# Writing out TensorE's and ScalarE's order in the weight fold of a recurrent-attention and mixture-of-experts kernel

## The chip, the core and the metric

The kernel runs on one core of a Trainium2 chip. The metric is the device time of one execution in microseconds (us), as the median of several runs.

## The reference

Three layers follow one another. The second has two matrices behind its product, and nothing between them, which is what the kernel's "fold" uses.

```python
# 1. recurrent attention, r,k,v,w: (4, 8, 768, 48), u: (8, 48)
for t in range(S):
    cur = einsum('bhd,bhe->bhde', u[None] * kt, vt)
    y[:, :, t] = einsum('bhd,bhde->bhe', rt, state + cur)
    state = wt[..., None] * state + einsum('bhd,bhe->bhde', kt, vt)
# 2. x: (3072, 384); w1, w2: (384, 1024); w3: (1024, 1024); w_out: (1024, 384)
x = (((x @ w1) * (x @ w2)) @ w3) @ w_out
# 3. eight experts, the best two of each token by noisy gate logits
logits = x @ w_gate + log1p(exp(x @ w_noise)) * noise
out[token] += weight[token, k] * (maximum(x @ e1[e], 0) @ e2[e])
```

## The kernel before, in words

**The fold.** w3 and w_out are multiplied with each other first: W = w3 @ [w_out | w_out @ (w_gate, w_noise)], 1024 rows of 400 columns. They arrive as 64-bit numbers. Every matrix is kept as a high and a low half, and a product takes three matmuls (`mm3`, lines 169 to 172: high x high at L170, high x low at L171, low x high at L172). W comes in two halves of four 128-row blocks; a half fills the PSUM banks PB[0] to PB[3] and is summed over eight blocks of w3, so there are sixteen blocks of w3, each with a set of twelve matmuls of 128x400 (`mm_w3`), and eight blocks of w_out.

**Conversion.** `cvt` (line 135) turns a loaded block into halves: ScalarE makes "top" (L145); a later `flush` (line 149) lets VectorE make the 32-bit number "z" (cvz, L154), ScalarE cast its high half "h" (L156), and the flush after that lets VectorE subtract to the low half "l" (L161). Each `cvt` calls `flush(1)` between its "top" and its entry into the queue; a flush first makes z and h of the block that waits and then l of the block before that.

**The gate exchange.** For each block of w_out TensorE transposes z (`wo_T`, L366), ScalarE copies the result out (woT, L368), TensorE multiplies it with the gate columns (`gate_cols`, L373), and ScalarE and VectorE split the 16 columns (`gate_split`, by `split`, L123 and L124). The set of block j needs both halves of these columns.

**Beside it.** A table `todo` holds steps by slot; pass u of the loop runs slot u - 24. In these slots lie the loads (`load_dt`, `load_na`, `load_w`, all issued by SP), the preparation of attention chunks 0 to 2 (`pre_steps`: pre_scan L193 on VectorE, pre_rec with Ln and Exp on ScalarE L202 and L203, further products on VectorE or POOL, pre_u on POOL L222 and L223, pre_c, and pre_d, eight ScalarE copies, L235), and chunks 0 and 1 themselves (`att_steps`: at_A L242 on TensorE, at_ov L247 on VectorE, at_T L252 with a ScalarE copy, at_kv L263 with sc and snew on VectorE L267 to L274 and the state's copies on ScalarE L278, at_y L302 with xh on ScalarE L308 and xl on VectorE L309). Slot -15 is that of chunk 0's pre_d and chunk 1's scan. Behind the loop the slots -5 to -1 follow, then the main loop over pairs of chunks, then the experts.

**What sets the order.** VectorE issues in the order in which the program is written, everywhere (line 78). The other engines' order is a planner's, made when the program is compiled: it takes the instructions by their place in the program and by when its model takes them to be ready, and so it may let a ready instruction pass one that waits. In the loop of lines 466 to 485 the set of block u - 3 is multiplied in pass u; the gate exchange of block u - 1 lies in pass u; W's first half is split in pass 10 at once, behind the eighth set.

Of the kernel before, what the change touches and what calls it, by code (L numbers as in the profile page):

```python
# [8 lines left out]
F32 = mybir.dt.float32  # L9
# [9 lines left out]
P = 128  # L19
B, H, S, D = 4, 8, 768, 48  # L20
DM, FF, E = 384, 1024, 8
# [8 lines left out]
XW = DM + 16  # L30
# [41 lines left out]
def tile_kernel(ctx: ExitStack, tc: tile.TileContext, dt, nat, w3t, wout, w1, w2, e1, e2, cf, ci, out):  # L72
    nc = tc.nc
    pe, act, dve, pool, sp = nc.tensor, nc.scalar, nc.vector, nc.gpsimd, nc.sync
# [6 lines left out]
    def f(ap):  # L81
        return ap.bitcast(F32)
# [17 lines left out]
    PB = [psum.tile([P, 512], F32, name=f"pb{i}") for i in range(8)]  # L100
# [9 lines left out]
    oneb = const.tile([P, P], BF16, name="oneb")  # L110
# [3 lines left out]
    att = attx.enter_context(tc.tile_pool(name="att", bufs=2))  # L114
# [4 lines left out]
    W0 = [wp.tile([P, 4, XW], F32R, name=x) for x in ("W0h", "W0l")]  # L119
    St = [att.tile([P, 4, 2 * D], F32, name=f"S{i}", bufs=1) for i in range(2)]  # L120

    def split(h, l, src, on=None):
        act.copy(out=h, in_=src)  # L123
        (on or dve).tensor_tensor(out=l, in0=src, in1=f(h), op=OP.subtract)  # L124
# [3 lines left out]
    def tops(n):  # L128

        pl, w, _ = CV  # L130
        TOP[:] = [pl.tile([P, w], I32, name=f"top{i}", bufs=1) for i in range(n)]
        for t in TOP:
            pool.memset(t, 0)
# [15 lines left out]
    def flush(n=2):  # L149
        for _ in range(n):  # L150
            low, LQ[:] = LQ[:], []
            while CQ:
                mid, t, z, h, l, post = CQ.pop()
                dve.scalar_tensor_tensor(z, mid, 13, t, op0=OP.logical_shift_right, op1=OP.bitwise_or)  # L154
                x = z.bitcast(F32)
                act.copy(out=h, in_=x)  # L156
                LQ.append((h, l, x))
                if post:
                    post(x)
            for h, l, x in low:  # L160
                dve.tensor_tensor(out=l, in0=x, in1=f(h), op=OP.subtract)  # L161

    def load64(rw, src):

        n = src.shape[-1]
        sp.dma_start(out=rw.bitcast(U16)[:, 1:4 * n + 1], in_=src.bitcast(U16))
        return rw[:, :2 * n + 2]

    def mm3(o, wh, wl, xh, xl, start, stop):
        pe.matmul(o, wh, xh, start=start, stop=False)  # L170
        pe.matmul(o, wh, xl, start=False, stop=False)  # L171
        pe.matmul(o, wl, xh, start=False, stop=stop)  # L172


    DT, NA, FG, RC, KT, RT, AM, KN, XH, XL, KS = ({} for _ in range(11))

    def load_dt(j):
        DT[j] = att.tile([P, NDT], F32, name="dtc")
        sp.dma_start(out=DT[j], in_=dt[j])
# [11 lines left out]
    def pre_scan(j):  # L191
        FG[j] = att.tile([P, 8 * (HC + 1)], F32, name="fg")
        dve.tensor_tensor_scan(out=FG[j], data0=DT[j][:, 8 * P:], data1=d1, initial=0.0,  # L193
                               op0=OP.mult, op1=OP.add)

    def pre_rec(j, step):

        fa = fgv(j)[:, :, 1:]
        if step == 0:
            RC[j] = att.tile([P, 8, HC], F32, name="rc", bufs=1)  # L200
            KT[j] = att.tile([P, 4, 2, HC], F32, name="kt")
            act.activation(out=RC[j], in_=fa, func=AF.Ln)  # L202
            act.activation(out=RC[j], in_=RC[j], func=AF.Exp, scale=-1.0)  # L203
        else:
            t = KT[j].rearrange("p a s i -> p (a s) i")
            off(j, 0).tensor_tensor(out=t, in0=fa, in1=RC[j], op=OP.mult)
            dve.scalar_tensor_tensor(RC[j], t, -2.0, RC[j], op0=OP.add, op1=OP.mult)

    def pre_k(j):
        k = DT[j][:, 4 * P:8 * P].rearrange("p (a s i) -> p a s i", s=2, i=HC)  # L210
        off(j, 1).tensor_tensor(out=KT[j][:, :, 0], in0=k[:, :, 0], in1=fgv(j)[:, 1::2, :HC], op=OP.mult)
        dve.scalar_tensor_tensor(KT[j][:, :, 1], k[:, :, 1], -1.0, RC[j][:, 0::2], op0=OP.mult, op1=OP.mult)

    def pre_r(j):
        RT[j] = att.tile([P, 4, 2, HC], F32, name="rt")
        r = DT[j][:, :4 * P].rearrange("p (a s i) -> p a s i", s=2, i=HC)
        dve.scalar_tensor_tensor(RT[j][:, :, 0], r[:, :, 0], -1.0, RC[j][:, 1::2], op0=OP.mult, op1=OP.mult)
        off(j, 2).tensor_tensor(out=RT[j][:, :, 1], in0=r[:, :, 1], in1=fgv(j)[:, 0::2, :HC], op=OP.mult)

    def pre_u(j):  # L220
        t = att.tile([P, DM], F32, name="rku", bufs=1)
        pool.tensor_tensor(out=t, in0=NA[j][:, :DM], in1=NA[j][:, DM:2 * DM], op=OP.mult)  # L222
        pool.tensor_tensor(out=t, in0=t, in1=c("u"), op=OP.mult)  # L223
        KS["u", j] = t

    def pre_c(j):
        t = KS["u", j]
        cc = att.tile([P, H], F32, name="cc")
        dve.tensor_reduce(out=cc, in_=t.rearrange("p (h d) -> p h d", h=H), axis=mybir.AxisListType.X, op=OP.add)
        KS["c", j] = cc  # L230

    def pre_d(j):
        AM[j] = att.tile([P, H, P], F32, name="am")
        for h in range(H):
            act.activation(out=AM[j][:, h], in_=ident, func=AF.Copy, scale=KS["c", j][:, h:h + 1])  # L235

    def at_A(j):
# [98 lines left out]
    def pre_steps(j):  # L336
        def p2():
            pre_k(j)
            pre_r(j)
            if j + 2 < NCH:  # L340
                load_dt(j + 2)

        return [lambda: pre_scan(j), lambda: pre_rec(j, 0), lambda: pre_rec(j, 1), p2, lambda: pre_u(j),
                lambda: pre_c(j), lambda: pre_d(j)]
# [4 lines left out]
    rawx, w3s, xo_, R1 = {}, {}, {}, {}  # L349
# [3 lines left out]
    def ld_raw(n=1):  # L353
        for _ in range(n):
            if order:
                k, u = order.pop(0)
                rawx[k, u] = load64(fold.tile([P, 1026], I32, name="rawf", bufs=7),
                                    wout[u] if k == "o" else w3t[u // 8, u % 8])

    def cv_wo(j):  # L360
        cvt(rawx["o", j], DM, woh[:, j, :DM], wol[:, j, :DM], post=lambda x: xo_.__setitem__(j, x))

    def wo_T(j):
        bank = PB[4 + j % 2]
        for kb in range(3):
            pe.transpose(bank[:, P * kb:P * kb + P], xo_[j][:, kb * P:kb * P + P], ident)  # L366
        xo_[j] = fold.tile([P, DM], F32, name="woT")
        act.copy(out=xo_[j], in_=bank[:, :DM])  # L368

    def gate_cols(j):  # L370
        g = bK[:, 256 + 32 * j:272 + 32 * j]
        for kb in range(3):
            pe.matmul(g, xo_[j][:, P * kb:P * kb + P], wgn[:, kb], start=kb == 0, stop=kb == 2)  # L373

    def gate_split(j):
        split(woh[:, j, DM:], wol[:, j, DM:], bK[:, 256 + 32 * j:272 + 32 * j])

    def cv_w3(u):
        w3s[u] = [fold.tile([P, 512], F32R, name=x, bufs=3) for x in ("w3h", "w3l")]
        cvt(rawx["3", u], 512, *w3s[u])  # L380

    def mm_w3(u):
        jb = u % 8
        for fb in range(4):
            s = slice(fb * P, fb * P + P)
            mm3(PB[fb][:, :XW], w3s[u][0][:, s], w3s[u][1][:, s], woh[:, jb, :], wol[:, jb, :], jb == 0, jb == 7)

    def load_w(m, fp):
        R1[m, fp] = load64(rawp.tile([P, 1538], I32, name="raw64"), (w1, w2)[m][fp])
# [19 lines left out]
    def at(slot, fn, *a):  # L409
        todo.setdefault(slot, []).append((fn, a))  # L410

    def run_todo(k):
        for fn, a in todo.pop(k, []):
            fn(*a)

    def start(j):
# [3 lines left out]
    PREL = {0: (-21, -20, -18, -17, -19, -16, -15), 1: (-15, -14, -13, -12, -14, -12, -11),  # L420
            2: (-10, -9, -4, -3, -6, -1, 0), 3: (1, 1, 4, 5, 3, 5, 6)}
# [16 lines left out]
            at(slot, cv_w, *k, i)  # L438
    for k, slot in WLD.items():
        at(slot, load_w, *k)  # L440
    for j in range(NCH):
        lo = ATT[j - 2][4] if 2 <= j < 6 else start(j - 2) + 4
        for i, fn in enumerate(pre_steps(j)):
            at(PREL[j][i] if j < 4 else max(lo, start(j) + PRE[i]), fn)
    for j in range(NCH):
        for i, fn in enumerate(att_steps(j)):
# [7 lines left out]
    ca = CF["u"][0]  # L454
    sp.dma_start(out=cft[:, :ca], in_=cf[:, :ca])
    ld_raw(6)
    tops(2)
    for t in St:
        pool.memset(t, 0.0)
# [1 line left out]
    pool.memset(d1.rearrange("p (a i) -> p a i", i=HC + 1)[:, :, :1], 1.0)  # L461
    pool.memset(zeros, 0.0)
    pool.memset(run, 0.0)
    pool.memset(oneb, 1.0)

    for u in range(19):
        if u < 8:
            cv_wo(u)
            ld_raw()
        if u < 16:  # L470
            cv_w3(u)
            ld_raw()
        elif u == 16:
            flush()
        if u > 2:
            mm_w3(u - 3)
        if 0 < u < 9:
            gate_cols(u - 1)
            gate_split(u - 1)
        if u < 8:  # L480
            wo_T(u)
        if u == 10:
            for fb in range(4):
                split(W0[0][:, fb], W0[1][:, fb], PB[fb][:, :XW])
        run_todo(u - 24)

    flush()
    foldx.close()
# [427 lines left out]
    if RMAX > 1:  # L916

        n = nc.values_load(rounds[0:1, E:E + 1], min_val=1, max_val=RMAX)  # L918
# [101 lines left out]
```

## Time and profile before

| | us |
|---|---|
| runs | 987.36, 987.98 (median), 988.5 |
| profiled execution, time | 987.58 |
| its span | 985.7 |
| TensorE busy (matmul) | 938.5 |
| VectorE busy | 444.7 |
| ScalarE busy | 424.2 |
| GpSimd busy | 345.3 |

The durations below come from the profiled execution. Its time is 1.88 us above its span, and 0.40 us below the median of the runs. PE is TensorE's matmul row, PEld its weight loads, DVE VectorE, ACT ScalarE, POOL GpSimd, SP the engine that issues loads. The end of a matmul is modelled, and matmuls overlap one another, so what a matmul costs is read from its start to the next start.

### The profile page before, as it was taken

What the parts mean: (1) busy time and instruction counts of PE and PEld (TensorE: products, weight loads), DVE (VectorE), ACT (ScalarE), POOL (GpSimd) and SP (SyncE); (2) the same over time, 40 slices, a digit from 0 to 9 for tenths busy, and PEclk for the clock granted to TensorE, in tenths of its full rate; (3) what the DMA queues carried; (4) which work ended last, traced back from release to release, by engine and by line L of the source; (5) the groups of instructions that cost most, each with busy time, mean ns of one, the idle gap of its engine ahead of it and who ended that gap; (6) DMA issues with size and microseconds to landing.
All of it is one profiled execution on the core that took longest, in us unless ns stands there. A gap on an engine that the chain in (4) does not pass through costs nothing. (4 is left out here: it accounts for less than half of the span.)

```text
span 985.7 us, 17863 instructions
## 1 busy us (share of the span) xinstructions
PE 938.5 (95%) x7219; PEld 865.0 (88%) x7219; DVE 444.7 (45%) x1059; ACT 424.2 (43%) x879; POOL 345.3 (35%) x281
## 2 busy tenths in 40 slices
PE   7898999999999999999899999999999999999993
PEld 6787899889899899899789879899898989999893
DVE  5779666646656648646244352221303122130310
ACT  6777545445345445444252343433414343342410
POOL 2122101312401410411304635655456565544421
PEclk9999999999999999999999999999999999999997
DMA  9845975544332322410212554534254353425012
GB/s 361 344 150 188 165 174 188 134 137 152 85 110 76 108 87 76 111 52 17 81 49 81 96 154 121 122 89 74 85 109 121 89 122 91 73 85 105 11 25 29
DMA packets 49179, 111.64 MB, mean 113 GB/s; under 512 B 17600, under 2 KB 32192, under 8 KB 49088
## 3 DMA queue, kind: packets, MB, share of 16 engines
q1 hardware_dynamic: 33472, 85.98, 28.5%
q0 software_dynamic: 12160, 19.72, 11.4%
q10 hardware_dynamic: 3456, 4.72, 1.4%
q8 instruction: 58, 0.95, 0.4%
q14 instruction: 33, 0.27, 0.1%
HBM read 88.12 MB, written 22.27 MB: 112 GB/s over the span
## 5 line engine op out<-in xcount | busy, mean ns | idle before, releaser
L170 PE MATMUL pb<-XTh,WAh 128*128 128x512 f32 (+1 forms) x384 | 132.8, 347 | 1.1 <-DVE HH L748 1.0
L171 PE MATMUL pb<-XTl,WAh 128*128 128x512 f32 (+1 forms) x384 | 131.5, 343 | 0.0
L170 PE MATMUL pb<-WBh,HH 128*128 128x384 f32 x384 | 130.1, 339 | 0.9 <-ACT HH L744 0.9
L172 PE MATMUL pb<-XTh,WAl 128*128 128x512 f32 (+1 forms) x384 | 130.8, 344 | 0.0
L171 PE MATMUL pb<-WBl,HH 128*128 128x384 f32 x384 | 129.6, 338 | 0.0
L172 PE MATMUL pb<-WBh,HH 128*128 128x384 f32 x384 | 129.4, 337 | 0.0
L771 POOL DMA_INDIRECT out<-ye,ti x56 | 87.7, 1567 | 110.3 <-ACT ye L762 95.3
L746 DVE SCALAR_TENSOR_TENSOR HH<-pb,HH 128x256 fp32r<-128x256 f32 (+1 forms) x128 | 71.4, 558 | 113.5 <-ACT HH L744 110.5
L222 POOL TENSOR_TENSOR rku<-natc 128x384 f32<-128x384 f32 x24 | 26.7, 1114 | 270.0 <-DMA natc<-nat 224.8
L744 ACT ACTIVATE HH<-pb 128x288 fp32r<-128x288 f32 (+1 forms) x128 | 64.4, 505 | 124.1 <-PE pb L172 115.8
L124 DVE TENSOR_TENSOR XTl<-pb,XTh 128x512 fp32r<-128x512 f32 (+1 forms) x48 | 25.6, 571 | 162.0 <-ACT XTh L123 143.1
L762 ACT ACTIVATE ye<-pb,ti 128x384 f32<-128x384 f32 x48 | 27.9, 581 | 161.4 <-PE pb L172 117.3
L170 PE MATMUL pb<-xh,WBh 128*128 128x256 f32 x288 | 83.8, 291 | 2.9 <-DVE pp L513 2.4
L170 PE MATMUL pb<-xh,WAh 128*128 128x256 f32 x288 | 83.6, 290 | 2.8 <-ACT xh L308 2.2
L172 PE MATMUL pb<-xh,WAl 128*128 128x256 f32 x288 | 82.0, 285 | 0.8 <-DVE WAl L161 0.7
L170 PEld LDWEIGHTS pb<-XTh,WAh 128*128 128x128 f32 x384 | 72.0, 188 | 11.8 <-DVE HH L746 1.8
L172 PE MATMUL pb<-xh,WBl 128*128 128x256 f32 x288 | 81.5, 283 | 1.0 <-DVE WBl L161 1.0
L171 PE MATMUL pb<-xl,WBh 128*128 128x256 f32 x288 | 82.2, 286 | 0.0
L171 PE MATMUL pb<-xl,WAh 128*128 128x256 f32 x288 | 82.0, 285 | 0.2
L172 PEld LDWEIGHTS pb<-XTh,WAl 128*128 128x128 f32 x384 | 71.7, 188 | 8.5 <-DVE WAl L701 0.2
L171 PEld LDWEIGHTS pb<-XTl,WAh 128*128 128x128 f32 x384 | 72.1, 188 | 7.9
L722 POOL DMA_INDIRECT xg<-x_rows,ti x56 | 54.6, 975 | 66.4 <-DMA ti<-slots 34.4
(168 smaller groups left out, 2254.7 us busy)
## 6 DMA issues: line engine op xcount, KB each, us to landing
raw<-e SPq DMA_DIRECT2D x32, 768.0 KB
dtc<-dt SPq DMA_DIRECT2D x24, 772.0 KB
natc<-nat SPq DMA_DIRECT2D x24, 640.0 KB
rawf<-w3t SPq DMA_DIRECT2D x16, 512.0 KB
raw<-w SPq DMA_DIRECT2D x8, 768.0 KB
x_rows<-xo ACTq DMA_DIRECT2D x24, 192.0 KB
out<-zeros SPq DMA_DIRECT2D x4, 1152.0 KB
rawf<-wout SPq DMA_DIRECT2D x8, 384.0 KB
```

The costliest lines, as they stand in the source:

```text
L124: (on or dve).tensor_tensor(out=l, in0=src, in1=f(h), op=OP.subtract)
L170: pe.matmul(o, wh, xh, start=start, stop=False)
L171: pe.matmul(o, wh, xl, start=False, stop=False)
L172: pe.matmul(o, wl, xh, start=False, stop=stop)
L222: pool.tensor_tensor(out=t, in0=NA[j][:, :DM], in1=NA[j][:, DM:2 * DM], op=OP.mult)
L722: pool.indirect_dma_start(out=XG[e, j][:rows_of(j)], out_offset=None, in_=x2d[:rows], in_offset=bass.IndirectOffsetOnAxis(ap=ti(e, j)[:, 0 ...
L744: act.activation(out=Hh[hf][:, ff], in_=bank, func=AF.Relu)
L746: dve.scalar_tensor_tensor(Hl[hf][:, ff], bank[:, :n], 0.0, f(Hh[hf][:, ff, :n]), op0=OP.max, op1=OP.subtract)
L762: act.activation(out=y[:n], in_=bank[:n], func=AF.Copy, scale=wt)
L771: ins = pool.indirect_dma_start(out=out, out_offset=bass.IndirectOffsetOnAxis(ap=ti(e, j)[:, 0:1], axis=0), in_=y[:n], in_offset=None, com ...
```

## The change

TensorE and ScalarE now also keep the written order within the fold; VectorE did and does. The loop is rewritten with 18 passes: gate_cols of block u - 2 and wo_T of block u - 1 come first, the set of block u - 2 last. wo_T's copy out of PSUM is a step of its own, behind both conversions. In the set of block 7 each bank of W's first half is split as soon as its three products are written. 36 products of a matrix of ones with itself stand at the start and 30 in pass 1, into PB[3], which the first set overwrites; the memset of that matrix moves to the front of POOL's work. pre_d of chunks 0 and 1 runs in two halves, in its slot and the next. The slot -6 runs behind the region.

```diff
-    def pre_d(j):
-        AM[j] = att.tile([P, H, P], F32, name="am")
-        for h in range(H):
+    def pre_d(j, part=None):
+        if not part:
+            AM[j] = att.tile([P, H, P], F32, name="am")
+        for h in range(H) if part is None else range(4 * part, 4 * part + 4):
...
+    def wo_copy(j):
         xo_[j] = fold.tile([P, DM], F32, name="woT")
-        act.copy(out=xo_[j], in_=bank[:, :DM])
+        act.copy(out=xo_[j], in_=PB[4 + j % 2][:, :DM])
...
             mm3(PB[fb][:, :XW], w3s[u][0][:, s], w3s[u][1][:, s], woh[:, jb, :], wol[:, jb, :], jb == 0, jb == 7)
+            if u == 7:
+                split(W0[0][:, fb], W0[1][:, fb], PB[fb][:, :XW])
+
+    def keep_busy(n):
+        for _ in range(n):
+            pe.matmul(PB[3][:, :P], oneb, oneb, start=True, stop=True)
...
+    for j in range(2):
+        at(PREL[j][6], pre_d, j, 0)
+        at(PREL[j][6] + 1, pre_d, j, 1)
...
+    pool.memset(oneb, 1.0)
     tops(2)
...
-    for u in range(19):
-        if u < 8:
-            cv_wo(u)
-            ld_raw()
-        if u < 16:
-            cv_w3(u)
-            ld_raw()
-        elif u == 16:
-            flush()
-        if u > 2:
-            mm_w3(u - 3)
-        if 0 < u < 9:
-            gate_cols(u - 1)
-            gate_split(u - 1)
-        if u < 8:
-            wo_T(u)
-        if u == 10:
-            for fb in range(4):
-                split(W0[0][:, fb], W0[1][:, fb], PB[fb][:, :XW])
-        run_todo(u - 24)
+    with tc.manual_schedule(engines={mybir.EngineType.PE, mybir.EngineType.Activation}):
+        keep_busy(36)
+        for u in range(18):
+            if 1 < u < 10:
+                gate_cols(u - 2)
+            if 0 < u < 9:
+                wo_T(u - 1)
+            if u < 8:
+                cv_wo(u)
+                ld_raw()
+            if 1 < u < 10:
+                gate_split(u - 2)
+            if u < 16:
+                cv_w3(u)
+                ld_raw()
+            elif u == 16:
+                flush()
+            if 0 < u < 9:
+                wo_copy(u - 1)
+            if u > 1:
+                mm_w3(u - 2)
+            elif u:
+                keep_busy(30)
+            run_todo(u - 24)
+    run_todo(-6)
```

## Rows read from the trace of the kernel before

**Rows 1.** The page, busy time of TensorE: busy us (share of the span), share of weight loads, VectorE, ScalarE, POOL follow on the page's own lines.
```profile
PE 938.5 (95%) x7219; PEld 865.0 (88%) x7219; DVE 444.7 (45%) x1059; ACT 424.2 (43%) x879; POOL 345.3 (35%) x281
```
**Rows 2.** Busy time of each engine in stretches: length, busy us (instructions) of each engine, TensorE's granted clock (1.00 is 2.4 GHz, 0.50 is 1.2 GHz), share of the DMA engines, GB/s.
```profile
6.00:13.00 7.00, 6.33 (x26) 5.90 (x27) 4.64 (x9) 5.35 (x13) 0.00 (x0) 1.00 1.03 398
13.00:41.20 28.20, 26.79 (x164) 22.72 (x162) 21.55 (x41) 21.84 (x50) 3.28 (x4) 1.00 0.97 375
...
70.20:112.00 41.80, 35.82 (x355) 31.38 (x358) 35.67 (x59) 28.43 (x64) 12.10 (x12) 1.00 0.62 206
```
**Rows 3.** Timeline of TensorE: the fold's first transposition and its last product. Columns: start, us, engine, line, operation, shapes, count, and in brackets the idle time before it and what ended it.
```profile
6.03 0.90 PE L366 MATMUL pb<-cft,cvz 128*128 128x128 f32 x3 [6.03 <-DVE cvz L154]
...
70.01 0.34 PE L172 MATMUL pb<-WBh,w3l 128*128 128x400 f32 x1
```
**Rows 4.** Timeline of TensorE at full speed: a transposition, products, a gate exchange, products.
```profile
13.86 0.49 PE L366 MATMUL pb<-cft,cvz 128*128 128x128 f32 x3
14.10 0.80 PE L170 MATMUL pb<-WBh,w3h 128*128 128x400 f32 x3
...
15.28 0.74 PE L373 MATMUL pb<-cft,woT 128*128 128x16 f32 x6
15.87 0.43 PE L172 MATMUL pb<-WBh,w3l 128*128 128x400 f32 x1
16.13 0.34 PE L171 MATMUL pb<-WBl,w3h 128*128 128x400 f32 x1
16.32 0.35 PE L172 MATMUL pb<-WBh,w3l 128*128 128x400 f32 x1
```
**Rows 5.** Timeline of TensorE: the steps of the attention chunks in the fold (36.75 to 50.14 chunk 0, from 57.40 on chunk 1; L302 of chunk 1 ran as many groups from 64.26 until the next product at 65.92).
```profile
36.75 0.71 PE L242 MATMUL pb<-rt,kt 48*128 48x128 f32 x6
39.06 0.93 PE L242 MATMUL pb<-rt,kt 48*128 48x128 f32 x10
50.14 1.08 PE L302 MATMUL pb<-am,natc 128*32 128x128 f32 x32
57.40 0.66 PE L252 MATMUL pb<-cft,kt 128*128 128x128 f32 x4
60.18 0.67 PE L263 MATMUL pb<-natc,kn 128*64 128x48 f32 x16
64.26 0.31 PE L302 MATMUL pb<-am,natc 128*32 128x128 f32 x3
65.92 0.45 PE L171 MATMUL pb<-WBl,w3h 128*128 128x400 f32 x1
```
**Rows 6.** Timeline of TensorE: products of the first set.
```profile
10.62 0.54 PE L172 MATMUL pb<-WBh,w3l 128*128 128x400 f32 x1
10.95 0.54 PE L171 MATMUL pb<-WBl,w3h 128*128 128x400 f32 x1
```
**Rows 7.** Who waited for whom, 0 to 70 us: us in total, times, longest.
```profile
ACT WBh L123 <- PE pb L373: 3.6, 7, 1.1
PE pb L170 <- DVE W0l L124: 1.9, 1, 1.9
```
**Rows 8.** Stretches of 2 us, columns as in rows 2.
```profile
42.00:44.00 2.00, 0.80 (x3) 0.79 (x4) 1.43 (x3) 2.00 (x6) 0.00 (x0) 0.83 1.02 424
44.00:46.00 2.00, 2.00 (x8) 1.98 (x7) 1.79 (x4) 2.00 (x5) 0.68 (x1) 0.50 1.02 420
46.00:48.00 2.00, 2.00 (x23) 1.67 (x21) 1.12 (x2) 1.07 (x2) 1.20 (x2) 0.81 0.75 311
...
84.00:86.00 2.00, 0.78 (x6) 0.81 (x7) 2.00 (x4) 1.49 (x5) 0.00 (x0) 1.00 0.53 221
```
**Rows 9.** Timeline of TensorE: the first product of block 7's set (seven further L170 and L171 follow) and its four L172.
```profile
37.38 0.44 PE L170 MATMUL pb<-WBh,w3h 128*128 128x400 f32 x1
...
40.22 0.98 PE L172 MATMUL pb<-WBh,w3l 128*128 128x400 f32 x4
```
**Rows 10.** Timeline of ScalarE at the start of the fold.
```profile
6.43 0.77 ACT L145 ACTIVATE top<-rawf 128x512 f16<-128x512 bf16 x1
7.07 0.45 ACT L368 COPY woT<-pb 128x384 f32<-128x384 f32 x1
7.42 0.64 ACT L145 ACTIVATE top<-rawf 128x384 f16<-128x384 bf16 x1
```
**Rows 11.** Timeline of ScalarE and VectorE: the split of W's first half, and two steps of chunk 0.
```profile
42.06 1.64 ACT L123 CAST W0h<-pb 128x400 fp32r<-128x400 f32 x4
42.57 2.02 DVE L124 TENSOR_TENSOR W0l<-pb,W0h 128x400 fp32r<-128x400 f32 x4 [0.74 <-ACT W0h L123]
...
49.44 0.36 DVE L274 TENSOR_TENSOR snew<-pb,sc 128x192 f32<-128x192 f32 x1
52.94 0.54 DVE L309 TENSOR_TENSOR xl<-pb,xh 128x384 fp32r<-128x384 f32 x1
```
**Rows 12.** Timeline of VectorE: a z while POOL multiplies at L222 (22.03 to 23.05), and a z, an l and a scan in line.
```profile
22.34 1.25 DVE L154 SCALAR_TENSOR_TENSOR cvz<-rawf,top 128x512 int32<-128x512 int32 x1 [0.83 <-ACT top L145]
...
54.61 0.68 DVE L154 SCALAR_TENSOR_TENSOR cvz<-rawf,top 128x512 int32<-128x512 int32 x1
55.21 0.68 DVE L161 TENSOR_TENSOR w3l<-cvz,w3h 128x512 fp32r<-128x512 f32 x1
55.81 1.23 DVE L193 TENSOR_TENSOR_SCAN fg<-dtc,d 128x520 f32<-128x520 f32 x1
```

More of the change, by code (lines that the diff above doesn't have):

```diff
@@ L440, in tile_kernel @@
         at(slot, load_w, *k)
+    for j in range(2):
+        at(PREL[j][6], pre_d, j, 0)
+        at(PREL[j][6] + 1, pre_d, j, 1)
     for j in range(NCH):
         lo = ATT[j - 2][4] if 2 <= j < 6 else start(j - 2) + 4
-        for i, fn in enumerate(pre_steps(j)):
+        for i, fn in enumerate(pre_steps(j)[:6 if j < 2 else 7]):
             at(PREL[j][i] if j < 4 else max(lo, start(j) + PRE[i]), fn)
@@ L463, in tile_kernel @@
     pool.memset(run, 0.0)
-    pool.memset(oneb, 1.0)
-    for u in range(19):
-        if u < 8:
-            cv_wo(u)
-            ld_raw()
-        if u < 16:
-            cv_w3(u)
-            ld_raw()
-        elif u == 16:
-            flush()
-        if u > 2:
-            mm_w3(u - 3)
-        if 0 < u < 9:
-            gate_cols(u - 1)
-            gate_split(u - 1)
-        if u < 8:
-            wo_T(u)
-        if u == 10:
-            for fb in range(4):
-                split(W0[0][:, fb], W0[1][:, fb], PB[fb][:, :XW])
-        run_todo(u - 24)
+    with tc.manual_schedule(engines={mybir.EngineType.PE, mybir.EngineType.Activation}):
[23 more added lines that the diff above has]
+    run_todo(-6)
     flush()
```

## The prediction

> **What bounds the kernel now.** I read the page first: TensorE is busy for 95% of the span [rows 1]. So the end moves by what TensorE loses or wins somewhere. The change touches the fold (the loop of lines 466 to 485), so the next views are the table by stretch [rows 2] and the ends of the fold [rows 3]. TensorE starts at 6.0 us; the fold's last product starts at 70.0 and makes room at 70.2; then comes a stage, to 112 us, with VectorE busy for 35.7 of 41.8 us and TensorE for 35.8. A fold that ends later or earlier moves everything behind it, unless that stage swallows it.
>
> How much of the fold is TensorE's own work? From start to next start: the first product of a set is 0.26, each other 0.18, so a set of twelve is 2.26 us; three transpositions 0.25; a gate exchange (six small products) 0.59 [rows 4]. The two attention chunks that run inside the fold, less the drain that overlaps the next instruction: L242 0.63 + 0.86, in one piece some 1.4; L252 0.41; L263 0.60; L302 1.01 for chunk 0 and, with two early ones, 2.0 for chunk 1 [rows 5]. Sum: 16 x 2.26 + 8 x 0.84 + 2 x (1.4 + 0.41 + 0.60) + 1.01 + 2.0 = 50.7 us. The fold takes 70.2 - 6.0 = 64.2, so **13.5 us are lost now**. Three places can be named. At first the products come 0.33 apart instead of 0.18, which is 1.2 GHz, although the granted-clock column says 1.00 there [rows 2, 6]. The eight gate exchanges make ScalarE wait 3.6 us in all for L373, and the split of W's first half makes TensorE wait 1.9 us for VectorE [rows 7]. Around that split the granted clock falls: 0.83, 0.50 and 0.81 in three stretches of 2 us, so 0.34 + 1.0 + 0.38 = 1.7 us are lost to it [rows 8]. Elsewhere TensorE loses little, and the trace shows why: where the low half of a weight block is late, the planner runs the products that need only the high half, goes on to L242, and brings the block's four L172 last [rows 5, 9].
>
> **The change part by part.** I count what TensorE loses in the new order. A "unit" is a pass of the changed loop.
>
> *Start.* The 36 dummy products need only the memset of oneb, which POOL now does first; the "top" buffers are cleared a fifth of a microsecond later, long before ScalarE's first use of them. The first transposition stays at 6.03. The first gate exchange moves to unit 2, and its operand is now copied behind seven ScalarE instructions. With ScalarE's steps (0.65 for a 512 "top", 0.52 for 384, that is 0.64 less the overlap of 0.12, 0.45 to the copy's end [rows 10]; 0.53 and 0.40 for the casts of 512 and 384, in proportion to 1.64 / 4 for W0's 400 columns [rows 11]) and the second "top" at 5.8 (an estimate: it ran at 6.43 behind a cast, and when its data landed isn't shown) the copy ends at about 9.6. TensorE loses 9.6 - 6.28 = **3.3**, which the 30 dummies fill. Between 9.2 (no load ever late) and 10.4 (0.8 later).
> That the clock is up by then is taken from the trace only in so far as it rose after TensorE had been working [rows 4, 6]; no row shows a dummy product. Were they without effect, some fifteen products would cost 0.15 more each: +2 us, an end of the range. The Trainium skill, "TensorE: Matmul & The Clock Gate", section "What's actually happening", calls the slow clock the default and says that activity releases it; by it the dummies do count and these 2 us don't arise.
>
> *Units 2 to 9, the exchanges.* gate_cols comes first, wo_T behind it, then the products. The wait left is the cast of the gate columns and its low half (0.17 each) behind gate_cols, and ScalarE stands in line there behind a cast that waits for VectorE. Between 0.1 (the bare chain beside wo_T) and 0.9 (with a scan, or an Ln and Exp, ahead). I take ScalarE's present wait, 3.6 / 8 = 0.45 each [rows 7]: **3.6**.
>
> *Products one unit earlier.* From unit 9 on, the low half of block u-2 is made in the very unit in which it is used: the flush makes "z" of block u-1 and then "l" of block u-2. VectorE keeps the written order, as before; now TensorE can't step around a late "l" either, so what stands ahead of "l" on VectorE stands ahead of TensorE. Durations: z 0.60 to the next start, l 0.68 to its end, scan 1.15 to the next start, its 1.23 less 0.08 [rows 12]; W0's cast 0.49 to its end and its low half 0.50 to the next start, from a quarter of the four; snew 0.36, xl 0.47 to the next start [rows 11].
> - Unit 9: gate columns and their low half end 1.1 into the unit, then z 0.60 and l 0.68: 2.4; the third product would start at 1.4. Loss **1.0**.
> - Unit 10: bank by bank only the last bank is left behind the products: drain 0.16, cast 0.49, low half 0.50. But chunk 1's scan (1.15) follows at once, then z 0.60 and l 0.68, with 0.1 of hops: 3.7. Two products (0.36) run meanwhile. Loss **3.3**, where it was 1.9.
> - Unit 12: VectorE holds snew, which waits for this chunk's L263, TensorE's last step of unit 11: drain 0.15 + 0.36 + 0.60 + 0.68 - 0.36 = **1.4**.
> - Unit 13: xl waits for xh (0.45, as the like-sized copy L368) and that for L302, the last of unit 12: 0.25 + 0.45 + 0.47 + 0.60 + 0.68 - 0.36 = **2.1**.
> - Units 14 to 17: nothing that waits for TensorE stands just ahead of an "l": 0.
>
> *The clock.* The stall of unit 10 is in the place of that of 42 us, longer, and follows on that of unit 9; the fall cost 1.7 there. At 84 to 86 us, behind a wait of 2.4 us, it stayed at 1.00 [rows 8]. I take **1.7**, the nearer row; the other end is 0.
>
> *Costing nothing.* wo_copy behind the cast, and pre_d in two halves: the same ScalarE instructions, with over 6 us of ScalarE idle in the stretch up to 41 [rows 2]; with that cover gone 0.35 a unit. Loads keep their slots, and SP waits for buffers as before; DMA is at 0.97 up to 41 us [rows 2], so a block can land late: between 0 and 2 us in all, I take 0. POOL's multiplications slow VectorE where they meet: a z took 1.25 instead of 0.68 [rows 12]; two such meetings ahead of an "l" would be +1.2, I take 0.
>
> **Sum.** Lost: 3.3 + 3.6 + 1.0 + 3.3 + 1.4 + 2.1 + 1.7 = 16.4. The fold ends at 6.0 + 50.7 + 16.4 = 73.1 instead of 70.2: **+2.9 us**. Behind it VectorE, busy for 35.7 of 41.8 us, also starts that stage later, so the delay is carried on. The planner will order that stage anew; TensorE's 6.0 us of idleness in it [rows 2] may come out 2.5 us better or worse. The profiled execution has 987.58 us for a span of 985.7, so it becomes 990.5; the median of the runs is 0.4 above it: **990.9 us**.
>
> **Rivals.**
> 1. *Faster: the low halves are in time.* If VectorE runs a unit ahead, the waits of units 9, 12 and 13 (4.5) vanish, and with less idleness the clock's fall (1.7): 10.2 lost, the fold ends at 66.9, **984.7 us**. For it: in units 2 to 8 VectorE has 2.2 us of conversions in a unit of 3.6. Against it: snew and xl wait for TensorE itself, which no head start takes away. It decides where "l" starts before its set's second product ends. Chance 0.2.
> 2. *No change.* The clock holds behind unit 10, as at 84 to 86, and the gate waits shrink to 0.3: 16.4 - 1.7 - 1.2 = 13.5, just what is lost now: **988.0 us**. Also if the stage behind the fold swallows the delay. Chance 0.28.
> 3. *Slower, as forecast*, 990.9; in its worse part the dummies don't raise the clock (+2) or loads are late (+2): up to 995.5. Chance 0.52.
>
> **How the numbers follow.** The likeliest case is the third. A measurement of this kernel tells about 0.2%, 2 us, from no change. The range takes in rival 1 and the late loads, 984.8 to 995.5; the slower case's own range is 989.5 to 995.5.
>
> **What would show it.** Right: products 0.18 apart from the first set on; TensorE waiting some 3 us at an L172 behind the W0 split, with a scan and one z ahead of its w3l on VectorE; two more waits of 1.4 and 2.1 us behind the first chunk's L263 and L302; the granted clock near 0.5 once, about 44; the fold's last L172 at 72 to 74 us. Wrong: w3l is not waited for, the last product stands before 69 us, or the stretch behind the fold has far less than 6 us of idleness.

## The result: 0.67% slower, and the loss is in the fold

| | before | after |
|---|---|---|
| runs | 984.67 to 990.87, median 987.98 (7) | 989.85 to 999.83, median 992.3 (7) |
| profiled execution, its span | 987.58, 985.7 | 992.64, 990.9 |
| the fold's last product starts at | 70.01 | 75.07 |
| the rest of the profiled time behind it | 917.57 | 917.57 |

The ratio of the changed kernel to the one before is 1.0067 with a 95% interval of 1.0043 to 1.0090: slower. The medians are 4.3 us apart, which is 0.44%; the ratio is taken over all the runs and need not be that of the medians. In the two profiled executions the fold ends 5.06 us later, and the whole time is 5.06 us longer. So the net loss is looked for ahead of 75 us.

The page of the kernel after, busy time of the engines (columns as in [rows 1]).

```profile
PE 941.0 (95%) x7285; PEld 870.6 (88%) x7285; DVE 443.8 (45%) x1059; ACT 425.1 (43%) x879; POOL 345.3 (35%) x281
```

TensorE's 66 further instructions are the dummies. More than that the totals can't show: 5 us are 0.5% of the span. The waits can.

Who waited for whom, TensorE up to 75 us: us in total, times, longest.

```profile
PE pb L172 <- DVE w3l L161: 6.8, 4, 3.2
PE pb L376 <- ACT woT L371: 2.2, 1, 2.2
PE pb L170 <- ACT WBh L123: 1.5, 4, 0.5
```

The first line is new. Before, no L172 of the fold waited for a low half; the largest wait behind the start was that of an L170 for the split of W's first half, 1.9 us [rows 7]. The timeline of TensorE shows the four places, and the start and end of the fold (after's L367 is before's L366, L371 its L368, L376 its L373, L396 the dummies).

```profile
1.01 3.78 PE L396 MATMUL pb<-oneb 128*128 128x128 bf16 x36 [1.01 <-POOL oneb L470]
6.06 0.55 PE L367 MATMUL pb<-cft,cvz 128*128 128x128 f32 x3 [1.27 <-DVE cvz L154]
6.44 1.84 PE L396 MATMUL pb<-oneb 128*128 128x128 bf16 x30
10.45 0.84 PE L376 MATMUL pb<-cft,woT 128*128 128x16 f32 x6 [2.16 <-ACT woT L371]
...
12.10 0.54 PE L171 MATMUL pb<-WBl,w3h 128*128 128x400 f32 x1
12.43 0.54 PE L172 MATMUL pb<-WBh,w3l 128*128 128x400 f32 x1
...
39.34 0.45 PE L172 MATMUL pb<-WBh,w3l 128*128 128x400 f32 x1 [0.75 <-DVE w3l L161]
44.96 0.45 PE L172 MATMUL pb<-WBh,w3l 128*128 128x400 f32 x1 [3.16 <-DVE w3l L161]
54.70 0.45 PE L172 MATMUL pb<-WBh,w3l 128*128 128x400 f32 x1 [1.11 <-DVE w3l L161]
60.18 0.45 PE L172 MATMUL pb<-WBh,w3l 128*128 128x400 f32 x1 [1.83 <-DVE w3l L161]
75.07 0.34 PE L172 MATMUL pb<-WBh,w3l 128*128 128x400 f32 x1
```

What stood ahead of the low half at the longest of them is read from VectorE's timeline, and so are the places of the last two: a z and an l queued behind snew, which waited 1.68 us for TensorE's L264 (before's L263), and behind an xl that itself waited 2.25 us for ScalarE's xh.

```profile
40.36 2.22 DVE L124 TENSOR_TENSOR W0l<-pb,W0h 128x400 fp32r<-128x400 f32 x4 [1.07 <-ACT W0h L123]
42.49 1.23 DVE L193 TENSOR_TENSOR_SCAN fg<-dtc,d 128x520 f32<-128x520 f32 x1
43.63 0.67 DVE L154 SCALAR_TENSOR_TENSOR cvz<-rawf,top 128x512 int32<-128x512 int32 x1
44.22 0.69 DVE L161 TENSOR_TENSOR w3l<-cvz,w3h 128x512 fp32r<-128x512 f32 x1
...
53.09 0.36 DVE L275 TENSOR_TENSOR snew<-pb,sc 128x192 f32<-128x192 f32 x1 [1.68 <-PE pb L264]
...
58.37 0.56 DVE L310 TENSOR_TENSOR xl<-pb,xh 128x384 fp32r<-128x384 f32 x1 [2.25 <-ACT xh L309]
58.84 0.68 DVE L154 SCALAR_TENSOR_TENSOR cvz<-rawf,top 128x512 int32<-128x512 int32 x1
59.44 0.68 DVE L161 TENSOR_TENSOR w3l<-cvz,w3h 128x512 fp32r<-128x512 f32 x1
```

The clock fell twice, and before only once [rows 8]. Stretches of 2 us, columns as in [rows 8]:

```profile
10.00:12.00 2.00, 1.55 (x10) 1.56 (x11) 1.33 (x4) 2.00 (x6) 0.00 (x0) 0.80 1.03 419
12.00:14.00 2.00, 2.00 (x7) 1.98 (x7) 1.84 (x4) 1.98 (x5) 0.00 (x0) 0.50 1.02 423
14.00:16.00 2.00, 2.00 (x14) 1.99 (x14) 0.00 (x0) 0.09 (x1) 0.00 (x0) 0.84 1.04 412
...
44.00:46.00 2.00, 1.04 (x4) 1.03 (x5) 2.00 (x4) 1.66 (x5) 0.00 (x0) 0.84 0.68 277
46.00:48.00 2.00, 2.00 (x8) 1.80 (x6) 0.11 (x1) 1.29 (x3) 0.60 (x1) 0.50 0.06 25
48.00:50.00 2.00, 2.00 (x23) 1.61 (x21) 1.39 (x2) 0.00 (x0) 1.53 (x2) 0.81 0.00 0
```

What is short of 1.00 in each row, times 2 us, adds up to 1.7 us for each fall. Each follows on one of TensorE's two longest waits, 2.16 and 3.16 us.

### The profile page after: what moved, and what is told of

Same layout as the page of the kernel before. It is cut to its first block, busy times and chain, and to the rows that moved or that the text cites. A ratio compares the mean times of both kernels' runs of the same rounds, so it can differ in the third digit from the quotient of the medians.

```text
span 990.9 us, 17975 instructions
## 1 busy us (share of the span) xinstructions
PE 941.0 (95%) x7285; PEld 870.6 (88%) x7285; DVE 443.8 (45%) x1059; ACT 425.1 (43%) x879; POOL 345.3 (35%) x281
## 5 line engine op out<-in xcount | busy, mean ns | idle before, releaser
L170 PE MATMUL pb<-XTh,WAh 128*128 128x512 f32 (+1 forms) x384 | 133.4, 349 | 0.1
L171 PE MATMUL pb<-XTl,WAh 128*128 128x512 f32 (+1 forms) x384 | 132.0, 344 | 0.0
L172 PE MATMUL pb<-XTh,WAl 128*128 128x512 f32 (+1 forms) x384 | 131.2, 345 | 0.0
L170 PE MATMUL pb<-WBh,HH 128*128 128x384 f32 x384 | 130.1, 339 | 0.9 <-ACT HH L763 0.9
L171 PE MATMUL pb<-WBl,HH 128*128 128x384 f32 x384 | 129.4, 338 | 0.0
L172 PE MATMUL pb<-WBh,HH 128*128 128x384 f32 x384 | 129.4, 337 | 0.0
L222 POOL TENSOR_TENSOR rku<-natc 128x384 f32<-128x384 f32 x24 | 26.9, 1119 | 282.2 <-DMA natc<-nat 233.1
L763 ACT ACTIVATE HH<-pb 128x288 fp32r<-128x288 f32 (+1 forms) x128 | 64.5, 505 | 124.4 <-PE pb L172 115.7
L170 PE MATMUL pb<-xh,WBh 128*128 128x256 f32 x288 | 84.3, 293 | 4.2 <-DVE pp L532 2.4
L170 PE MATMUL pb<-xh,WAh 128*128 128x256 f32 x288 | 83.8, 291 | 3.8 <-ACT xh L309 2.3
L172 PE MATMUL pb<-xh,WAl 128*128 128x256 f32 x288 | 82.3, 286 | 0.8 <-DVE WAl L161 0.7
L172 PE MATMUL pb<-xh,WBl 128*128 128x256 f32 x288 | 81.9, 284 | 1.0 <-DVE WBl L161 1.0
L171 PE MATMUL pb<-xl,WBh 128*128 128x256 f32 x288 | 82.7, 287 | 0.0
L171 PE MATMUL pb<-xl,WAh 128*128 128x256 f32 x288 | 82.2, 285 | 0.1
L170 PEld LDWEIGHTS pb<-XTh,WAh 128*128 128x128 f32 x384 | 72.5, 189 | 10.8 <-DVE HH L765 2.1
L172 PEld LDWEIGHTS pb<-XTh,WAl 128*128 128x128 f32 x384 | 72.2, 189 | 8.5 <-DVE WAl L720 0.2
L171 PEld LDWEIGHTS pb<-XTl,WAh 128*128 128x128 f32 x384 | 72.7, 189 | 7.9
```

What stands on the lines that cost most here:

```text
L763: act.activation(out=Hh[hf][:, ff], in_=bank, func=AF.Relu)
```

## The experiments

Two theories. **Theory A:** the loss comes from the sets being multiplied one pass earlier, so that the low half is made in the pass that uses it; whatever stands ahead of "l" on VectorE then stands ahead of TensorE. **Theory B (rival):** the loss comes from taking the planner's freedom away, so that TensorE can't step around what is late. Smaller questions: what the dummies are worth, and the rewritten exchange.

The runs came in four sets, in which before itself took 987.98 (beside after), 990.52 (e1 to e4), 988.71 (e7 to e9, a2) and 966.87 us (f1 to f3) at the median. The last three sets ran on three different chips (1, 12 and 4). So every time is set against before in its own set, and only ratios are compared across sets. Runs with a single execution have no interval. "End of the fold" is the start of its last product, in one profiled execution.

| kernel | order written out | set in pass u | ratio to before, 95% | end of the fold | waits for l, us |
|---|---|---|---|---|---|
| before | no | u - 3 | 1 | 70.01 | none listed |
| after | yes | u - 2 | 1.0067 (1.0043 to 1.0090) | 75.07 | 6.8 |
| e1_planner | no | u - 2 | 1.0055 (1.0022 to 1.0087) | 72.16 | 2.6 |
| e4_lag3 | yes | second half u - 3 | 1.0008 (0.9981 to 1.0035) | 71.85 | 2.9 |
| e9_before_strict | yes | u - 3 | 0.9952 (0.9929 to 0.9974) | 69.36 | 1.0 |
| f3_strict_again | yes | u - 3 | 0.9969 (0.9952 to 0.9985) | 68.67 | 1.0 |
| f2_strict_lag2 | yes | u - 2 | 1.0044 (1.0024 to 1.0065) | 76.85 | 7.3 |
| f1_strict_dummies | yes | u - 3 | 0.9957 (0.9939 to 0.9974) | 67.87 | 1.0 |

**e1_planner: the changed loop without the written order.**

```diff
-    with tc.manual_schedule(engines={mybir.EngineType.PE, mybir.EngineType.Activation}):
+    with ExitStack():
```

> The changed kernel with its new loop, dummies, bank-by-bank split and halved pre_d, but TensorE and ScalarE left to the planner as before. Theory (the written order makes TensorE stand behind late low halves): the four waits of TensorE at an L172 for w3l (6.8 us in the changed kernel) are gone or below 2 us together, the fold's last product starts at 69 to 72 us instead of 75.07, the time is 986 to 990. Rival (the new loop and the dummies themselves cost it: first exchange at 10.45 and a fall of the clock at 12): the last product stays at 73.5 us or later, the time at 991 or more.

994.3 us against 990.52. The planner does step around the late halves again, as the waits of TensorE up to 78 us show:

```profile
PE pb L171 <- DVE WBl L124: 4.5, 5, 2.3
PE pb L172 <- DVE w3l L161: 2.6, 2, 1.7
```

The waits for w3l shrink from 6.8 to 2.6 us, but 4.5 us for the low half of the gate columns appear. Its fold ended 2.1 us later than that of before, its median is 3.8 us longer. Neither expectation came true as a whole: the end of the fold, 72.16, is near the theory's 69 to 72, the waits are above its 2 us, and the time is the rival's. Part of the time goes with the clock: before's runs in this set were granted 0.985 on average, these 0.980, and the four of them at 0.985 or more took 987.83 to 992.54 us, the eight below it 992.35 to 1001.6. So giving the freedom back does not bring the time back: theory B is hurt, not yet refuted, since the planner's order is another one altogether.

**e9_before_strict: the loop of before, with TensorE's and ScalarE's order written out and nothing else.**

```diff
-    for u in range(19):
-        ...
+    with tc.manual_schedule(engines={mybir.EngineType.PE, mybir.EngineType.Activation}):
+        for u in range(19):
+            ...
```

> The kernel before with one thing of the change alone: its own loop (sets of block u-3, products ahead of the exchange, W's half split at once) in the written order on TensorE and ScalarE. In this order l of block u-3 is made a pass ahead of its set, and woT's copy has a set's length of TensorE work behind it. Theory (it is the set one unit earlier that makes TensorE stand behind w3l, not the written order as such): no wait for w3l over 1 us, the split still costs 1 to 2 us; walking the durations along that order puts the fold's last product at 64.5 to 66.5 us with one fall of the clock, up to 68 with two; the time is 2 to 5 us below the kernel before. Rival (the written order itself costs, since the planner can no longer step around late halves): the last product at 71 or later, the time at or above that of the kernel before.

984.5 us (979.09 to 987.72, 12 runs) against 988.71: **faster** than before by 4 us, ratio 0.9952. Theory B predicts the opposite sign and falls. The last product came at 69.36, not at 64.5 to 68: the time was foreseen, the place not. A second run of the same kernel, f3_strict_again, shows one place where the order helps. Its TensorE timeline around the split of W's first half:

```profile
39.14 0.34 PE L172 MATMUL pb<-WBh,w3l 128*128 128x400 f32 x1
39.41 1.16 PE L242 MATMUL pb<-rt,kt 48*128 48x128 f32 x16
40.50 0.66 PE L252 MATMUL pb<-cft,kt 128*128 128x128 f32 x4
41.70 0.45 PE L170 MATMUL pb<-WBh,w3h 128*128 128x400 f32 x1 [0.55 <-DVE W0l L124]
```

Before, the planner had run L242 and L252 around the late low halves and kept four L172 for last, so the banks were full only behind 40.22 [rows 9], and the split was waited for with nothing left to do: 1.9 us [rows 7] and a fall of the clock [rows 8]. In the written order the last product of the set starts at 39.14, L242 and L252 cover the split, 0.55 us of waiting is left, and the granted clock stays at 1.00 there. The spared fall is not what the medians gain, though. In both profiled executions a fall came soon behind the fold instead (84 to 90 us in e9_before_strict, 78 to 82 in f3_strict_again), where before had its next one at 200. And over all runs the mean granted clock is that of before in the same set: 0.985 and 0.985 for e9_before_strict, 0.990 and 0.991 for f3_strict_again.

> The kernel of e9_before_strict once more, for its scatter and beside the other two on one chip: 984 to 985.5 us, 3 to 5 us below before; last product of the fold between 68.5 and 70 us; TensorE waits for low halves 1.0 us in all.

962.54 us against 966.87 in the same set, 4.3 us below before; last product at 68.67; waits for w3l 1.0 us. The difference is as expected, the ratio 0.9969 lies in the interval of the first run; the 984 to 985.5 us do not carry over to a set in which before itself is 2% shorter.

**f2_strict_lag2: that kernel with the sets one pass earlier, and with them the split of W's first half; the slot -6 runs behind the region, as in the changed kernel.**

```diff
-        for u in range(19):
+        for u in range(18):
...
-            if u > 2:
-                mm_w3(u - 3)
+            if u > 1:
+                mm_w3(u - 2)
...
-            if u == 10:
+            if u == 9:
                 for fb in range(4):
                     split(W0[0][:, fb], W0[1][:, fb], PB[fb][:, :XW])
...
+    run_todo(-6)
```

> The loop of before with the written order (as e9_before_strict) in which only one thing is moved: the set of block u - 2 is multiplied in pass u (before: u - 3), with W's first split in pass 9 and 18 passes. The exchange, its copy, the dummies and pre_d are as before. Theory 'the sets one unit early are the loss': TensorE waits for low halves 6 to 7 us in all (e9_before_strict 1.0) behind the split of W, L263 and L302, with one or two falls of the clock; less about 1 us won at the start, the last product comes at 74 to 76.5 us and the time is 4 to 6 us above e9_before_strict. Rival 'the rest of the rewritten loop (exchange first, bank by bank, dummies) is the loss': the waits for low halves stay under 3 us, the last product is within 1.5 us of 69.4.

969.24 us, where f3_strict_again in the same set took 962.54: +6.7 us, above the 4 to 6 expected, and the last product at 76.85 is 0.35 behind the expected stretch. Its waits, in the places of those of the changed kernel:

```profile
38.26 0.45 PE L172 MATMUL pb<-WBh,w3l 128*128 128x400 f32 x1 [1.21 <-DVE w3l L161]
43.90 0.70 PE L172 MATMUL pb<-WBh,w3l 128*128 128x400 f32 x1 [3.16 <-DVE w3l L161]
56.46 0.45 PE L172 MATMUL pb<-WBh,w3l 128*128 128x400 f32 x1 [1.11 <-DVE w3l L161]
61.94 0.45 PE L172 MATMUL pb<-WBh,w3l 128*128 128x400 f32 x1 [1.83 <-DVE w3l L161]
76.85 0.34 PE L172 MATMUL pb<-WBh,w3l 128*128 128x400 f32 x1
```

This is theory A alone, and it gives the changed kernel's waits to a hundredth of a microsecond in three places of four. For the two profiled executions the sum closes as well: between their folds lie 76.85 - 68.67 = 8.2 us. Waits for l: + 7.3 - 1.0 = 6.3; wait for the split: -0.55; one long fall of the clock (0.50 from 44 to 52 us, 5.1 us in all from its rows of 2 us): +5.1; the first product at 9.97 instead of 12.47: -2.5. Together 8.35. The long fall is not in the medians: at a granted clock of 0.985 the kernel took 972.14 (the profiled execution) to 975.3 us in four runs, at 0.988 to 0.991 in the other eight 968.03 to 969.39, still some 6 us above f3_strict_again, whose runs were granted 0.989 to 0.992. So the sets one pass earlier cost time at like clock too; of these 6 us the waits and the start account for 6.3 - 0.55 - 2.5 = 3.2 by the two profiles, and where the rest lies isn't shown. The run also bears on an edit that no run tried alone: here the split is written behind the whole set and not bank by bank, and the wait behind it is the same 3.16 us.

**e4_lag3: the changed kernel with the old distance in the second half only.**

```diff
-        for u in range(18):
+        for u in range(19):
...
-            if u > 1:
+            if u > 10:
+                mm_w3(u - 3)
+            elif 1 < u < 10:
                 mm_w3(u - 2)
```

> The changed kernel, strict order kept, but the second half's sets one unit later (block u-3 from pass 11 on, no set in pass 10, 19 passes), so that l is made a unit ahead of its use as before. Theory: the waits for w3l of units 12 and 13 (1.11 and 1.83) go or fall below 1 together, that of block 8 falls from 3.16 to some 2.2 because the first chunk's L243 and L253 run meanwhile; the last product of the fold at 71.5 to 73 instead of 75.07, the time 2 to 4 us below the changed kernel's. Rival (the loss is in the exchanges and the start, not in the lag): the last product stays within 1 us of 75.07.

991.67 us against 990.52, ratio 1.0008: no difference from before that can be told, and not as slow as the changed kernel. The waits for w3l fall from 6.8 to 2.9 us: 0.75 stays, 3.16 becomes 1.48, of 1.11 and 1.83 together 0.69 is left. The end of the fold falls from 75.07 to 71.85, within the expected 71.5 to 73; less the clock's falls (one here, two there) that is from 71.65 to 70.15. By the ratios the time is 0.6% below the changed kernel's, where 2 to 4 us, 0.2 to 0.4%, were expected.

**e3_scan_later: chunk 1's scan one slot later.**

```diff
-    PREL = {... 1: (-15, -14, -13, -12, -14, -12, -11),
+    PREL = {... 1: (-14, -14, -13, -12, -14, -12, -11),
```

> The changed kernel with chunk 1's scan one slot later, behind the l of block 8 instead of ahead of it. Theory (VectorE's written order is what TensorE waits for in unit 10): the wait there falls from 3.16 us by the scan's 1.15 to 2.0, the other waits stay (0.75, 1.11, 1.83), the last product of the fold moves from 75.07 to some 73.9, or to 72.2 if the shorter wait also spares the fall of the clock. Rival (that wait has its length from ScalarE or a load): it stays above 2.7 us.

The wait behind the split fell from 3.16 to 2.03 us, by the scan's 1.15, as read from VectorE's queue:

```profile
43.93 0.46 PE L172 MATMUL pb<-WBh,w3l 128*128 128x400 f32 x1 [2.03 <-DVE w3l L161]
52.79 0.68 PE L172 MATMUL pb<-WBh,w3l 128*128 128x400 f32 x1 [1.73 <-DVE w3l L161]
59.84 0.70 PE L172 MATMUL pb<-WBh,w3l 128*128 128x400 f32 x1 [1.83 <-DVE w3l L161]
```

But the next wait grew from 1.11 to 1.73, and in this execution the clock fell three times (10 to 16, 52 to 58, 58 to 64 us: 5.1 us). The fold ended at 76.18, 71.0 less the clock (75.07 and 71.65 for after), and the one time was 995.9. The mechanism is right; the last product was expected at 72.2 to 73.9, and that the edit brings time is not shown.

**e2_dummies64, e7_no_dummies, e8_before_dummies, f1_strict_dummies: what the dummies are worth.**

```diff
 e2:  -                keep_busy(30)
      +                keep_busy(64)
 e7:  -        keep_busy(36)
      -            elif u:
      -                keep_busy(30)
 e8:  loop of before, +    keep_busy(36) ahead of it
 f1:  e9_before_strict, +        keep_busy(36) ahead of the loop
      +            if u < 3:
      +                keep_busy(20)
```

> The changed kernel with 64 dummy products instead of 30 in pass 1, which at the 0.061 us that they took reach from 6.44 to 10.35, just to the first gate exchange at 10.45. Theory (the clock fell at 11.6 to 14.4 because TensorE idled for 2.2 us ahead of the exchange): no fall there, the first two sets run 0.18 apart, the last product of the fold moves from 75.07 to 73.3 to 73.8. Rival (the fall has another cause, or the later units stand behind the loads anyway): the fall stays, or it goes and the last product stays within 0.5 us of 75.07.

> The changed kernel without its 66 dummy products. Theory (the dummies' speed is lost again in the wait ahead of the first exchange, where the clock fell): the first two sets run at half speed for about as long, and the fold's last product stands at 74.5 to 76 with two falls or a slow start and one fall, as with them (75.07). Rival (the dummies are worth the 2 us that their absence was priced at): it stands at 77 or later.

> The kernel before with the 36 dummy products at the start, and the memset of ones first on POOL; nothing else. Theory (the chain through ScalarE, VectorE and the loads sets the first units, the slow clock of TensorE only in part): the first products run 0.18 apart or fall back once, the fold's last product moves from 70.01 to between 68.5 and 70. Rival (the 6 us at half speed are worth their full 2.7 us): it stands below 68.

> The loop of before with TensorE's and ScalarE's order written out (as e9_before_strict), and dummy products: 36 at the start and 20 at the end of each of the passes 0 to 2. In e9_before_strict the products of the first sets stood 0.33 us apart until 16.5 us. Theory 'the slow start is lost time': some 17 products become 0.15 us cheaper, the fold's last product comes at 67 to 68 us instead of 69.36, and the time is 1.5 to 2.5 us below that of e9_before_strict. Rival 'the start is bound by the chain of conversions, not by TensorE': the products go faster and then wait, or a later stretch falls to half speed instead; the last product stays within 0.7 us of 69.4 and the time within 1 us.

Without any dummy the fold of the changed kernel ended at 75.30, with those of the change at 75.07, with 64 in pass 1 at 75.73 (times of one execution each: 996.88, 992.64, 993.17). That is the theory of e7_no_dummies and the rival of e2_dummies64. But the falls of the clock lay elsewhere in each: one at 44 to 50 without dummies, two with those of the change, two with 64, at 38 to 44 and 46 to 50. Less 1.7 us for each fall the ends are 73.6, 71.65 and 72.3: at equal falls the dummies would be worth 1 to 2 us, which single executions don't show. With 64, the clock did not fall at 12 us, and TensorE's wait for the gate columns (L170 for WBh, L123) grew from 1.5 to 2.7 us: what was faster was waited for later. In the loop of before, one execution with dummies ended its fold at 71.23 where 68.5 to 70 was expected: a miss, with a planner's order that waited 2.4 us for w3h, and with products still 0.33 apart at 12.35. In the written order of before they do lift the start. In f1_strict_dummies the products are 0.18 apart from the first on, where those of f3_strict_again, in the same set, are 0.33 apart up to 16.29:

```profile
13.15 0.43 PE L170 MATMUL pb<-WBh,w3h 128*128 128x400 f32 x1
13.42 0.34 PE L171 MATMUL pb<-WBl,w3h 128*128 128x400 f32 x1
13.60 0.34 PE L172 MATMUL pb<-WBh,w3l 128*128 128x400 f32 x1
```

And in f3_strict_again:

```profile
12.96 0.54 PE L171 MATMUL pb<-WBl,w3h 128*128 128x400 f32 x1
13.29 0.54 PE L172 MATMUL pb<-WBh,w3l 128*128 128x400 f32 x1
```

The first set takes 2.28 us instead of 4.14, but starts 0.68 later (13.15 against 12.47), and the fold's end gains 0.80: 67.87 against 68.67. By the Trainium skill, "TensorE: Matmul & The Clock Gate", section "What's actually happening", activity releases the slow clock; these rows agree, 0.18 against 0.33. In e8_before_dummies 36 dummies at the start alone did not do it. The medians are 961.75 and 962.54 us, 0.8 apart, with runs that overlap: at most a microsecond, as the rival expected of the time; the end of the fold is the theory's 67 to 68. Its median is the lowest of its set, 5 us below before (0.9957, 0.9939 to 0.9974), though not told apart from the written order alone.

**a2_after_again: the changed kernel a second time.**

> The changed kernel once more, unchanged. Theory: the four waits for w3l come out within 0.2 us of 0.75, 3.16, 1.11 and 1.83, and the end of the fold less 1.7 us for each fall of the granted clock within 0.7 us of 71.65; the falls may lie elsewhere and be one to three, so the last product at 73.3 to 77. Rival (the fold's end is that of one execution and its waits are chance): waits or this difference elsewhere by over 1 us.

995.54 us; last product at 74.30, 72.6 less its one fall of the clock (1.7 us at 44 to 48), where 71.65 was expected: 0.95 off. The four waits are 0.76, 3.15, 1.10 and 1.83: they belong to the order. The first fall does not. Here the dummies of pass 1 ran at half speed, 3.41 us instead of 1.84, the idle time ahead of the first exchange was 0.23 us instead of 2.16, and the clock did not fall at 12.

```profile
6.48 3.41 PE L396 MATMUL pb<-oneb 128*128 128x128 bf16 x30
10.11 0.91 PE L376 MATMUL pb<-cft,woT 128*128 128x16 f32 x6 [0.23 <-ACT woT L371]
```

## Why the prediction was right, point by point

**The verdict and its size.** 990.9 was forecast, slower; 992.3 was measured, 1.4 us more. In the profiled executions the miss is larger, 992.64 against 990.5: the start (+0.8) and a second fall of the clock (+1.7), less 0.4 of the waits and the rest. That the median came nearer is luck; the seven runs lie between 989.85 and 999.83. The last product was to stand at 72 to 74 us and stood at 75.07. The named mechanism, low halves made in the pass that uses them, is the one that f2_strict_lag2 shows by itself. The working has small slips that decide nothing: the steps up to the first exchange add up to 9.4, not 9.6; rival 1's 984.7 lies just outside the range that is said to take it in; and 990.9 with both additions of 2 us is 994.9, not 995.5.

**The waits, unit by unit.** Forecast 1.0, 3.3, 1.4 and 2.1, together 7.8; measured 0.75, 3.16, 1.11 and 1.83 as idle time, together 6.8. From start to start it is about 7.5, as the product ahead of each wait is modelled 0.34 long where the next could start 0.18 behind it. The instructions ahead of the low halves were those named: the scan and one z behind the split, snew, and xl behind xh. e3_scan_later took the scan out of its place and 1.13 us went with it.

**The start: mis-sized.** The first exchange was forecast at 9.6, between 9.2 and 10.4; it came at 10.45, and 4.1 us were lost instead of 3.3. ScalarE's timeline has the reason, three "top"s that wait for their loads, 1.24 us together, of which the forecast had put in some 0.4 (the second "top" at 5.8 instead of the end of the first at 5.4):

```profile
6.04 0.78 ACT L145 ACTIVATE top<-rawf 128x512 f16<-128x512 bf16 x1 [0.63 <-DMA rawf<-w3t]
7.41 0.64 ACT L145 ACTIVATE top<-rawf 128x384 f16<-128x384 bf16 x1 [0.23 <-DMA rawf<-wout]
8.89 0.78 ACT L145 ACTIVATE top<-rawf 128x512 f16<-128x512 bf16 x1 [0.38 <-DMA rawf<-w3t]
```

**The clock: one fall was forecast, two came.** The first stood in the place that the dummies were to protect. Thirty of them took 1.84 us at full speed, not the 3.3 us that were to be filled, and left 2.16 us of idleness. "Products 0.18 apart from the first set on" was therefore wrong in this execution and right in a2_after_again. +1.7 us. Over the runs the clock takes part as well: the seven of the changed kernel were granted 0.982 on average, those of before 0.985 in the sets of e1 and e9 (in this set its clocks are not on record), and the two lowest of the seven, 0.975 and 0.977, are the two longest, 999.83 and 996.77 us. How much of the 4.3 us between the medians comes with the clock isn't shown.

**The exchanges and the rest.** Lost in all: 75.07 + 0.18 - 6.06 - 50.7 = 18.5 us, forecast 16.4. Less the start (4.1), the waits (7.5) and the clock (3.4), 3.5 are left for exchanges and everything else, forecast 3.6. Listed as waits are 1.5. Read from each exchange's first product to the set's first product, the eight take 9.8 us where their own work (0.59 each and seven transpositions of 0.25) is 6.5: 3.3 us, so the term was well sized. One of them, 1.40 instead of 0.84:

```profile
18.58 0.74 PE L376 MATMUL pb<-cft,woT 128*128 128x16 f32 x6
...
19.98 0.45 PE L170 MATMUL pb<-WBh,w3h 128*128 128x400 f32 x1 [0.29 <-ACT WBh L123]
```

**The stage behind the fold.** Its own reordering was allowed 2.5 us either way; the time behind the last product is 917.57 in both. TensorE's idleness in it went from 6.0 [rows 2] to 6.9 us, as the row of the equal stretch of the kernel after shows (columns as in [rows 2]):

```profile
75.26:117.06 41.80, 34.89 (x330) 30.59 (x330) 36.18 (x60) 28.95 (x65) 12.42 (x12) 1.00 0.64 225
```

The 0.9 is one wait that the prediction did not have: the first L170 behind the fold waits 1.52 us for "ac", where it waited 0.58 before. That the equality is so exact is chance: by its rows of 2 us the clock cost 6.8 us behind the fold in before's execution and 8.5 in this one, so something else there came out shorter by as much; and in the other profiles of the first three sets of runs (all but f1 to f3) the same difference lies between 916.79 and 921.58.

**What the prediction had not seen.** It took the present order as the measure and asked what a written one would lose against it. The written order by itself wins 4 us at the median (e9_before_strict, f3_strict_again); one place where TensorE waits less is shown, the split of W's first half. The change is thus a sum of two terms of opposite sign. By the ratios, the order alone is worth -0.3 to -0.5%, and the sets one pass earlier +0.75% on top of it (1.0044 / 0.9969). Both together stand 0.44% above before (f2_strict_lag2), the changed kernel 0.67%. The intervals overlap; whether the rewritten exchange and the dummies cost the other 0.2% is left open.

**Still open.** In the profiles e9_before_strict's fold ends only 0.65 us ahead of that of before, while the medians differ by 4.2 us. No profile of before from the same set tells whether the rest lies in the fold's scatter or behind it; the mean granted clock, the same for both in that set, does not explain it. And what decides whether the clock falls behind a given wait was not settled (below).

## What to carry to other kernels

When a producer-consumer pair is brought a step closer, list what the producer's in-order engine holds between the two, above all steps that wait for the consumer itself; each is a wait for the consumer. Writing an order out and shortening a distance are two changes: measure them apart, because here one gained what the other lost. Work that only keeps an engine busy is worth having only if what it speeds up is not waiting for something else.

## What the runs showed of the hardware

- **The clock's fall is not fixed by a wait's place or length.** In the changed kernel it followed on waits of 2.16 and 3.16 us, and in before on one of 1.9; in before it stayed at 1.00 behind a wait of 2.4 us [rows 8]. In e3_scan_later it stayed at 1.00 behind the wait of 2.03 us and fell behind those of 1.73 and 1.83. In a2_after_again the wait of 3.15 us brought the same 1.7 us; in f2_strict_lag2 a wait of 3.16 us brought one fall of 5.1 us, at 0.50 for four stretches in a row although TensorE was busy in all of them:

```profile
44.00:46.00 2.00, 2.00 (x6) 1.98 (x7) 1.25 (x2) 1.55 (x3) 0.34 (x1) 0.50 0.88 363
46.00:48.00 2.00, 2.00 (x9) 1.52 (x10) 1.13 (x1) 0.00 (x0) 1.92 (x3) 0.50 0.08 31
48.00:50.00 2.00, 2.00 (x18) 1.77 (x17) 0.71 (x2) 0.00 (x0) 1.84 (x2) 0.50 0.00 0
50.00:52.00 2.00, 2.00 (x9) 1.98 (x8) 1.03 (x3) 1.31 (x3) 0.00 (x0) 0.50 0.00 0
```

- **Half speed at the start is not in the granted-clock column.** In f3_strict_again the first products stand 0.33 us apart up to 16.29, in a column that says 1.00; the spacing of like instructions tells it.
- **A dummy product is cheap and of no fixed price**: 30 took 1.84 us in one execution of the changed kernel and 3.41 us in another.
- **Sets of runs differ by 2%**: before took 966.87 us in the set on chip 4 and 987.98 to 990.52 in the others (two of them on chips 1 and 12), more than any edit here was worth.
